# Two order changes in a fused attention and expert kernel: the sixth block product before the second, and nine memsets behind the first query halves

## The chip, the cores and the metric

The kernel runs on one core of a Trainium2 chip. The metric is the device time of one execution in microseconds (us). Engines are named as in the profile: PE is TensorE's matmul, PEld its weight load, DVE is VectorE, ACT is ScalarE, POOL is GpSimd, SP is SyncE. Each of them works its own queue of instructions in order and waits on semaphores for the others.

## What is computed

A block-sparse attention feeds a mixture of eight experts whose gate is normalised by eight Sinkhorn rounds.

```python
# attention: batch 4, heads 8, sequence 768, head size 64; block 32, window 16
k_sum = k.reshape(B, H, nb, block, D).max(axis=3)
v_sum = v.reshape(B, H, nb, block, D).mean(axis=3)
scores_l = where(|pos_q - pos_k| < window, scale * q @ k.T, -1e9)
scores_s = scale * q @ k_sum.T + log(block)
a = softmax(concat(scores_l, scores_s))
x = a @ concat(v, v_sum)                     # then laid out as 3072 x 512
# experts: 8 of them, 512 -> 1024 -> 512
P = exp(x @ w_gate - max)
for _ in range(8):
    P /= P.sum(1); P /= P.sum(0); P *= N / E
out = sum over e of P[:, e] * (relu(x @ w1[e]) @ w2[e])
```

## The kernel before

**Attention stage.** The work is cut into 16 pairs of heads, four to a batch. Pairs 0 to 3 (batch 0) are further cut into two halves of the queries. For each of these, POOL loads keys, the first half of the queries and values (`load_pair`, L256, L274, L268). PE transposes keys (`tr`, L296) and queries (`tr_qh`, L283); ACT or DVE copies the result out of PSUM (L195); DVE takes key maxima by block (`key_max`, L312); PE sums the values by block (`block_sums`, L326), and DVE copies these (`block_out`, L333); PE makes scores (`scores_h`, L318), ACT their exponentials (L442), DVE masks them (`masks_h`, L447 and L452); PE makes scores against the key maxima (`summaries`, L404), ACT their exponentials (L425). PE then multiplies with the values (`values_h`, L463), DVE takes the reciprocal of the sums (L493) and normalises (L494), PE transposes to `xT` (`to_xT`, L501) and ACT or DVE copies that (L195). Pairs 4 to 15 do the same for whole pairs, with `E_e` and `V_e` as operands for the keys near a tile's edge; SP copies the near values into `V_e` (`near_values`, L346 and L348).

The order of all this is not written out. Each step is a `Unit` with its engine, a cost in us, what it depends on and a priority, and `Plan.order` builds the program from them: it goes forward in its own time, and on each engine takes the unit that can start first, the lower priority number first where several can. The costs are constants in the source (`add("DVE", 1.6, late_constants, ...)`), and the order it makes is fixed in the program. Until expert 0's first result the plan also fills long PE waits with pairs of idle matmuls (`keep_busy`, L539).

`late_constants` (L588 to L593) is one such unit. It holds nine memsets on DVE: the two `E_e` tiles, the two `V_e` tiles with two small ones each, and `col_en`, the matrix that sums columns over partitions in the Sinkhorn rounds. It has priority 5.5, behind pairs 0 to 3's first halves (0 to 3) and ahead of the second halves (10 to 13).

Expert 0 is done without block products, as filler for PE (`expert0`: hidden products L199, projections L204), as soon as all four pairs of a batch (of batch 0: of one half) are in `xT`. Its units have the highest priority numbers. The gate (`gate`, L515 and L519) follows each batch. After the last batch come the Sinkhorn rounds (L1056 to L1077, their matmul at L1069), with the first groups of expert 1 and the last of expert 0 beside them.

**Steady period.** For experts 1 to 7 both layers are split two by two and done with seven block products in place of eight, with sums of blocks made beforehand on DVE (`x_sum`, `w1_sum`, `w2_sum`). Layer 1 works in groups (expert e, 512 of the 1536 tokens of a half, 128 of the 512 hidden columns of a half): `group` gives its steps, p1 to p7 on PE (L867, two matmuls of 512 columns each) and what is done with them. Layer 2 works in pairs (`pair`), q1 to q7 on PE (L873, four matmuls of 256 columns each), four groups behind. A step's result is accumulated in PSUM and copied to start another, so the steps wait for each other:

```python
def seed(): B["g"] = ...; nc.scalar.copy(out=B["g"][:], in_=B["a"][:])     # after p1
def c5():   B["c5"] = ...; nc.scalar.copy(out=B["c5"][:], in_=B["b"][:])   # after p5
def p6():   product1(e, i, j, B["g"], "S2", "T2", False)
def c2():   B["c2"] = ...; nc.scalar.copy(out=B["c2"][:], in_=B["g"][:])
def p2():   product1(e, i, j, B["a"], "A12", "B21", False)
def r11():  relu("ACT", h[:, A11, :], B["a"][:])
def c12():  plus(h[:, A21, :], B["b"][:], B["c2"][:])                      # after p3
def p7():   product1(e, i, j, B["g"], "S3", "T3", False)                   # after c2
```

p6 and p2 both need the seed. p7 accumulates on bank g, so it has to wait until c2 has copied it. The order of the period is written out by hand, as a list of `do(...)` calls in the main loop (n over groups, 80 periods). By engine it comes to:

- PE: q1 p1 p5 q5 p2 p6 q6 p3 p7 q2 q4 q3 p4 q7
- ACT: r21 (of the group before), c1 (L980), seed (L886), c5 (L894), r11 (L190), c2 (L901), v6 (L992); for expert 1 also two scalings (`scale0`, L965), with one operation on POOL behind them (L967)
- DVE: ya, yb of the pair before (L1010), v5 (L817, xy), s4 (L814), in some periods the sums for later groups, then c12 and c22 (L817, hf from pb and pg), r12 (L928), r22 (L931), s1 (L817), s3 and s2 (L814)

s3 needs r11's and r12's results; q6 needs v5; p3 needs c5; p4 needs c22; q3 and q7 need v6. The first four groups are in the plan of the attention stage (`bridge`) and have an order of their own.

Of the kernel before, what the change touches and what calls it, by code (L numbers as in the profile page):

```python
# [33 lines left out]
class Plan:  # L34
# [12 lines left out]
    def add(self, eng, cost, fn, deps=(), prio=0.0, opens=(), uses=(), lag=0.0):  # L47
        u = Unit(eng, cost, fn, [d for d in deps if d is not None], prio, list(opens), lag)
        for b in list(opens) + list(uses):
            b.users.append(u)  # L50
        if uses and eng != "PE":
            u.prio -= 100.0
        self.waiting.append(u)
        return u
# [62 lines left out]
def kernel(  # L117
# [21 lines left out]
    PB = H // 2  # L139
# [31 lines left out]
    def load_w1(e, i):  # L171
        t = w1s[e, i] = wpool.tile([128, KD, 2, 128], FP16, tag="w1", name="w1", bufs=5)
        for h in range(2):
            f = h * (F // 2) + 128 * i
            nc.gpsimd.dma_start(out=t[:, :, h, :],  # L175
                                in_=moe_w1[e].rearrange("(dk p) f -> p dk f", p=128)[:, :, f:f + 128])
# [7 lines left out]
    def load_w2(e):  # L184
        w2s[e] = wpool.tile([128, KF, DM], FP16, tag="w2", name="w2")
        nc.gpsimd.dma_start(out=w2s[e][:], in_=moe_w2[e].rearrange("(fk p) d -> p fk d", p=128))
# [34 lines left out]
    if True:  # L221
# [16 lines left out]
        add = plan.add  # L238
# [357 lines left out]
        U = {}  # L596
# [52 lines left out]
        def pair_half(i, h, prio):  # L649
            if h:  # L650
                query_half(i, 1, prio)
            n = PB * h + i
            hold = U["A", PB - 1, 0] if h else None
            buf = Buffer("s")
            U["S", i, h] = add("PE", 0.36, lambda: scores_h(i, h),
                               [U["kT", i, 0], U["kT", i, 1], hist("mk", n - 3), hold], prio, opens=[buf])
            U["X", i, h] = add("ACT", 1.0, lambda: score_exp_h(i, h), [U["S", i, h]], prio, uses=[buf])
            U["mk", i, h] = add("DVE", 0.78, lambda: masks_h(i, h),
                                [U["X", i, h], U["band"], hist("A", n - NEH)], prio)
            tag = "a" if h else "m"  # L660
            buf = Buffer(tag)
            U["ss", i, h] = add("PE", 0.22, lambda: summaries(i, h, tag),
                                [U["km", i], U["kT", i, 1], hist("A", n - 2), hold], prio, opens=[buf])
            U["sx", i, h] = add("ACT", 0.46, lambda: summary_exp(i, h), [U["ss", i, h]], prio, uses=[buf])
            buf = Buffer("a")
            U["A", i, h] = add("PE", 0.65, lambda: values_h(i, h),
                               [U["mk", i, h], U["sx", i, h], U["Vs", i]], prio, opens=[buf])
            U["no", i, h] = add("DVE", 0.68, lambda: normalize(i, h), [U["A", i, h], hist("xt", n - 2)],
                                prio, uses=[buf])
            buf = Buffer("a")  # L670
            U["xt", i, h] = add("PE", 0.18, lambda: to_xT(i, h), [U["no", i, h]], prio, opens=[buf])
            U["x", i, h] = add({"ACT": 0.46, "DVE": 0.5}, 0, lambda: x_out(U["x", i, h].on, i, h),
                               [U["xt", i, h]], prio, uses=[buf])
# [37 lines left out]
        def expert0(t0, xs):  # L711
            key, n = t0, len(halves)
            halves.append(key)
            pr = 1000.0 + n
            w = [U["w1", i] for i in range(2)]
            evac, old = [], [U.get(("pj", halves[n - 2], c)) for c in range(HG)] if n >= 2 else []
            for f in range(KF):
                buf = Buffer("m")

                def fn(f=f):  # L720
                    at["hp", key, f] = hidden0(key, t0, f)
                m = U["hd", key, f] = add("PE", 0.67, fn, xs + [w[f // 4]] + old, pr + f * 0.01, opens=[buf])

                def ev(f=f):
                    relu(U["rl", key, f].on, at["h", key][:, f, 0:HS], at.pop(("hp", key, f))[:, 0:HS])
                U["rl", key, f] = add({"ACT": 0.5, "DVE": 0.56}, 0, ev, [m], -1.0, uses=[buf])
                evac.append(U["rl", key, f])
                zero.extend([m, evac[-1]])
            for c in range(HG):
                buf = Buffer("m")  # L730
                p0 = add("PE", 0.88, lambda c=c: project0(key, c, 0), evac[0:4] + [U["w2"]],
                         pr + 0.1 + c * 0.02, opens=[buf])
                p1 = add("PE", 0.88, lambda c=c: project0(key, c, 1), evac[4:8] + [p0],
                         pr + 0.11 + c * 0.02, uses=[buf])
                U["pj", key, c] = p1

                def ev(c=c):
                    copy(U["yo", key, c].on, out_acc[:, t0 // 128 + c, :], at.pop(("yp", key, c))[:])
                U["yo", key, c] = add({"ACT": 0.58, "DVE": 0.68}, 0, ev, [p1], -1.0, uses=[buf])
                zero.extend([p0, p1, U["yo", key, c]])  # L740
# [23 lines left out]
        for i in range(PB):  # L764
            pair_start(i, i)
            pair_half(i, 0, i)
        add("DVE", 1.6, late_constants, [U["mk", 0, 0]], 5.5)
        expert0(0, [U["x", i, 0] for i in range(PB)])
        for i in range(PB):
            pair_half(i, 1, 10 + i)  # L770
# [28 lines left out]
    if True:  # L799
# [27 lines left out]
        def x_sum(j, n):  # L827
            m = {w: moving1(w, j) for w in "B11 B12 B21 B22 T1 T2 T3 T4".split()}
            sub(*[m[w] for w in (("T1", "B12", "B11"), ("T2", "B22", "T1"), ("T3", "B22", "B12"),
                                 ("T4", "B21", "T2"))[n]])  # L830
# [15 lines left out]
        def w1_sums(e, i):  # L846
            for n in range(4):
                w1_sum(e, i, n)
# [8 lines left out]
        def w2_sum(e, n):  # L857
            if n == 0:
                ws2[e] = extra[0].tile([128, 3, FH, DH], FP16, tag="ws2", name="ws2", bufs=2)
            m = {w: moving2(w, e) for w in "B11 B12 B21 B22 T1 T2 T3 T4".split()}  # L860
            sub(*[m[w] for w in (("T1", "B12", "B11"), ("T2", "B22", "T1"), ("T3", "B22", "B12"),
                                 ("T4", "T2", "B21"))[n]])
# [277 lines left out]
        for n in range(LAG, len(groups)):  # L1140
            g0, q0 = g, q
            g = group(*groups[n])
            q = pair(*groups[n - LAG])
            e, j, i = groups[n]
            later = e + 1 < E

            def do(*names):
                for nm in names:
                    f = g.get(nm) or q.get(nm)
                    if f is not None:  # L1150
                        f()

            def do0(*names):
                for nm in names:
                    f = g0.get(nm) or q0.get(nm)
                    if f is not None:
                        f()

            if j == 1 and i == 1 and later:
                load_w2(e + 1)  # L1160
                load_w1(e + 1, 0)
            do("q1", "p1")
            do0("r21")
            do("c1", "seed")
            do0("ya", "yb")
            do("p5", "c5")
            if n == LAG:
                w2_sum(1, 0)
                w2_sum(1, 1)
            do("q5", "v5")  # L1170
            do0("s4", "fin")
            if n == LAG:
                w2_sum(1, 2)
                w2_sum(1, 3)
            do("p2", "r11")
            if n < 2 * LAG:
                x_sum(2, n - LAG)
            if j == 2 and i > 1 and later:
                w1_sums(e + 1, i - 2)
            if e > 1 and j == 0 and i < 2:  # L1180
                w1_sums(e, i + 2)
            if j == 2 and i < 2 and later:
                w2_sum(e + 1, i)
            if e > 1 and j == 0 and i > 1:
                w2_sum(e, i)
            do("p6", "c2")
            do("q6", "v6")
            do("p3", "c12")
            do("p7", "c22", "r12")
            do("q2", "q4", "q3")  # L1190
            do("r22", "s1", "s3", "p4", "s2", "q7")
            if groups[n - LAG][0] == 1:
                do("scale0")
            if j == 2 and i < 3 and later:
                load_w1(e + 1, i + 1)
# [53 lines left out]
```

The softmax here doesn't subtract the row's maximum and nothing guards it: scores larger than these inputs give would overflow.

## Time and profile before

| what | value |
|---|---|
| median of 4 runs | 686.23 us (685.9 to 686.6) |
| profiled execution | 686.6 us, span of the core 684.9 us |
| PE | busy 671.9 us (98% of the span), 5191 matmuls |
| DVE | 590.5 us (86%) |
| ACT | 406.7 us (59%) |
| POOL | 134.5 us (20%) |
| chain that ended last | PE 85%, DVE 11%, issue 2%, DMA 1% |
| mean granted TensorE clock | 0.996 |
| first hidden product of expert 0 | 27.06 us |
| first product of the steady loop | 175.4 us |

The span is the time from the first to the last instruction of the core; the execution is 1.7 us longer. A matmul's row in a timeline shows its start and a modelled end; matmuls overlap, so distances between starts tell more than busy shares. A row of the timeline gives start, length, engine, line, operation and tiles; in square brackets stands the idle time of the engine before it, and what ended that.

### The profile page before, as it was taken

Reading aid. Unit: us, or ns where it says so; the run is one execution under the profiler, and the core shown is the slowest. Engines: PE = TensorE matmul, PEld = TensorE weight load, DVE = VectorE, ACT = ScalarE, POOL = GpSimd, SP = SyncE. Lnnn points to the kernel's source line nnn. Section 1 sums busy time; section 2 is a strip of 40 time slices with the busy share of each in tenths; the row PEclk is TensorE's granted clock in tenths of the full one; section 3 lists DMA queues with packets and bytes.
Section 4 is the critical chain, followed back from the end, with each engine's and each line's share of the span. In section 5 each row is a group of like instructions: output and inputs, shape, how many; then the busy total and the mean of one; then the engine's idle time right before and its main releaser. Section 6 shows DMA issues by size and latency. Waiting matters only on the chain.

```text
span 684.9 us, 13584 instructions
## 1 busy us (share of the span) xinstructions
PE 671.9 (98%) x5191; PEld 439.1 (64%) x5191; DVE 590.5 (86%) x1445; ACT 406.7 (59%) x784; POOL 134.5 (20%) x177
## 2 busy tenths in 40 slices
PE   7999999999999999999999999999999999999996
PEld 4666665545666666666666666666666666666665
DVE  6879988688699997999889988998899888998886
ACT  4677877555677765555555555555555555555551
POOL 8699720122203120100101010201010101100000
PEclk9999999999999999999999999999999999999999
DMA  9999990000324013220513050403131051301224
GB/s 115 190 143 142 117 124 7 1 1 0 53 26 42 7 23 56 24 24 1 78 16 32 1 78 1 48 1 57 22 31 17 7 72 16 33 1 47 78 93 154
DMA packets 113617, 33.90 MB, mean 50 GB/s; under 512 B 99984, under 2 KB 110736, under 8 KB 113552
## 3 DMA queue, kind: packets, MB, share of 16 engines
q0 software_dynamic: 104672, 26.22, 40.6%
q1 hardware_dynamic: 8352, 6.80, 3.3%
q8 instruction: 41, 0.67, 0.4%
q14 instruction: 24, 0.20, 0.1%
q10 hardware_dynamic: 528, 0.02, 0.0%
HBM read 52.45 MB, written 6.29 MB: 86 GB/s over the span
## 4 chain that ended last, share of the span: by engine, by line
PE 85%; DVE 11%; issue 2%; DMA 1%; POOL 0%; ACT 0%; DVEq 0%; ACTq 0%
PE xy L873 32%; PE pg L867 14%; PE pb L867 10%; PE pa L867 9%; PE yps L204 6%; PE hps L199 6%; DVE hf L817 3%; DVE out_acc L1010 2%; PE tkq L299 1%; PE sg L318 1%; DVE hf L928 1%; DMA vx<-in_v_dram 1%; DVE hf L814 1%; PE tx L501 1%; PE vs L326 1%
## 5 line engine op out<-in xcount | busy, mean ns | idle before, releaser
L873 PEld LDWEIGHTS <-hf 128*128 128x128 f16 x2352 | 229.7, 98 | 99.3 <-issue 5.3
L873 PE MATMUL xy<-w,hf 128*128 128x256 f16 x1312 | 183.3, 272 | 0.0
L873 PE MATMUL xy<-ws,hf 128*128 128x256 f16 x984 | 147.6, 272 | 1.5
L190 ACT ACTIVATE hf<-pg 128x512 f16<-128x512 f32 x84 | 50.2, 597 | 158.1 <-PE pg L867 158.1
L1010 DVE SCALAR_TENSOR_TENSOR out_acc<-xy,P_sb,out_acc 128x512 f32<-128x512 f32 x164 | 115.0, 743 | 1.7 <-PE xy L873 1.7
L814 DVE TENSOR_TENSOR hf<-hf 128x512 f16<-128x512 f16 x252 | 98.9, 420 | 2.9
L867 PE MATMUL pa<-xT,w 128*128 128x512 f16 x336 | 99.9, 379 | 0.0
L817 DVE TENSOR_TENSOR hf<-pb,c 128x512 f16<-128x512 f32 x84 | 57.9, 689 | 35.6 <-ACT xy L992 31.5
L867 PEld LDWEIGHTS <-w 128*128 128x128 f16 x672 | 65.6, 98 | 28.9 <-issue 0.3
L175 POOL DMA_DIRECT2D w<-in_moe_w_dram x56 | 41.9, 760 | 185.6 <-PE pg L867 157.3
L867 PEld LDWEIGHTS <-ws 128*128 128x128 f16 x504 | 49.3, 98 | 41.9
L190 ACT ACTIVATE hf<-pa 128x512 f16<-128x512 f32 x84 | 50.1, 597 | 19.2 <-PE pa L867 18.9
L817 DVE TENSOR_TENSOR hf<-pg,c 128x512 f16<-128x512 f32 x84 | 57.0, 679 | 0.1
L886 ACT COPY pg<-pa 128x512 f32<-128x512 f32 x84 | 47.9, 570 | 4.8
L867 PE MATMUL pg<-xTs,w 128*128 128x512 f16 x168 | 50.0, 379 | 0.1
L867 PE MATMUL pb<-xTs,ws 128*128 128x512 f16 x168 | 50.0, 379 | 0.0
L867 PE MATMUL pb<-xT,ws 128*128 128x512 f16 x168 | 50.0, 379 | 0.0
L867 PE MATMUL pg<-xTs,ws 128*128 128x512 f16 x168 | 50.0, 379 | 0.0
L894 ACT COPY c<-pb 128x512 f32<-128x512 f32 x84 | 49.8, 592 | 0.2 <-ACT pg L886 0.2
L867 PE MATMUL pg<-xT,w 128*128 128x512 f16 x168 | 49.8, 377 | 0.0
L199 PE MATMUL hps<-xT,w 128*128 128x384 f16 x256 | 49.4, 326 | 0.0
L901 ACT COPY c<-pg 128x512 f32<-128x512 f32 x84 | 48.7, 580 | 0.1
(136 smaller groups left out, 850.9 us busy)
## 6 DMA issues: line engine op xcount, KB each, us to landing
w<-in_moe_w_dram POOLq DMA_DIRECT2D x8, 1024.0 KB, 9.4
w<-in_moe_w_dram POOLq DMA_DIRECT2D x56, 128.0 KB, 3.6
out_dram<-out_acc SPq DMA_DIRECT2D x22, 256.0 KB, 2.0
qst<-in_q_dram POOLq DMA_DIRECT2D x32, 96.0 KB, 5.5
vx<-in_v_dram POOLq DMA_DIRECT2D x16, 192.0 KB, 6.3
kst<-in_k_dram POOLq DMA_DIRECT2D x24, 96.0 KB, 5.8
w<-in_moe_w_dram POOLq DMA_DIRECT2D x2, 512.0 KB, 8.7
kst<-in_k_dram POOLq DMA_DIRECT2D x4, 192.0 KB, 5.2
```

The lines of the kernel that those rows point to most:

```text
L175: nc.gpsimd.dma_start(out=t[:, :, h, :], in_=moe_w1[e].rearrange("(dk p) f -> p dk f", p=128)[:, :, f:f + 128])
L190: nc.scalar.activation(out=out, in_=in_, func=AF.Relu, bias=0.0, scale=1.0)
L199: nc.tensor.matmul(hp[:, 0:n], lhsT=w1s[e][:, dk, 128 * f:128 * (f + 1)], rhs=xT[:, dk, t0:t0 + n], start=(dk == 0), stop=(dk == KD - 1))
L204: nc.tensor.matmul(yp[:], lhsT=h[:, f, c * 128:(c + 1) * 128], rhs=w2s[e][:, f, :], start=(f == 0), stop=(f == KF - 1))
L814: nc.vector.tensor_tensor(out=out, in0=in0, in1=in1, op=ALU.subtract)
L817: nc.vector.tensor_tensor(out=out, in0=in0, in1=in1, op=ALU.add)
L867: nc.tensor.matmul(bank[:], lhsT=w[:, dk, :], rhs=x[:, dk, :], start=start and dk == 0, stop=dk == KH - 1, skip_group_check=True)
L873: nc.tensor.matmul(bank, lhsT=a(f)[:, 128 * c:128 * (c + 1)], rhs=w[:, f, :], start=start and f == 0, stop=f == FH - 1, skip_group_check=True)
L886: nc.scalar.copy(out=B["g"][:], in_=B["a"][:])
L894: nc.scalar.copy(out=B["c5"][:], in_=B["b"][:])
L901: nc.scalar.copy(out=B["c2"][:], in_=B["g"][:])
L1010: nc.vector.scalar_tensor_tensor(out=acc, in0=src, scalar=P_sb[:, t, e:e + 1], in1=acc, op0=ALU.mult, op1=ALU.add)
```

## The change

Two places. In the plan of the attention stage, `late_constants` depends on the masks of the last pair's first half (`PB` is 4) in place of the first pair's, and its cost in the plan is 2.4 in place of 1.6. In the steady loop, the calls for p6 and c2 and those for p2 and r11 change places; what lies between them (sums on DVE) stays where it is. The first groups of expert 1 in `bridge` are not touched.

```diff
         for i in range(PB):
             pair_start(i, i)
             pair_half(i, 0, i)
-        add("DVE", 1.6, late_constants, [U["mk", 0, 0]], 5.5)
+        add("DVE", 2.4, late_constants, [U["mk", PB - 1, 0]], 5.5)
         expert0(0, [U["x", i, 0] for i in range(PB)])
...
             if n == LAG:
                 w2_sum(1, 2)
                 w2_sum(1, 3)
-            do("p2", "r11")
+            do("p6", "c2")
             if n < 2 * LAG:
                 x_sum(2, n - LAG)
...
             if e > 1 and j == 0 and i > 1:
                 w2_sum(e, i)
-            do("p6", "c2")
+            do("p2", "r11")
             do("q6", "v6")
             do("p3", "c12")
             do("p7", "c22", "r12")
```

In the built program the steady part differs by the swap alone on PE and ACT (and in what s3 waits for). In the attention stage the planner makes another order of units on PE, DVE and ACT from about the second pair on; the same steps are in it, with two idle matmuls fewer. The queues of POOL and SP keep their order.

## The prediction

> **What bounds the kernel now.** I read the page first (PE busy in 98% of a 684.9 us span), then the table by stages, because a share over the whole span mixes stages with different limits.
>
> ```profile
> 0.00:15.00 15.00, 11.50 (x120) 5.93 (x120) 10.32 (x76) 6.42 (x9) 12.88 (x22) 0.98 1.18 108
> 15.00:30.00 15.00, 14.77 (x219) 9.31 (x216) 11.36 (x29) 9.39 (x16) 9.22 (x12) 0.91 1.45 196
> 30.00:60.00 30.00, 30.00 (x361) 18.90 (x358) 24.39 (x62) 23.07 (x37) 27.18 (x32) 1.00 2.30 146
> ...
> 202.00:255.00 53.00, 51.94 (x351) 34.01 (x349) 50.85 (x112) 39.60 (x77) 12.83 (x17) 1.00 0.18 18
> 255.00:300.00 45.00, 45.00 (x312) 30.40 (x311) 39.46 (x92) 24.08 (x50) 4.45 (x6) 1.00 0.38 46
> 300.00:400.00 100.00, 100.00 (x691) 67.30 (x689) 90.54 (x211) 56.13 (x116) 8.29 (x11) 1.00 0.19 22
> ```
>
> After the stretch, its length and then PE, PEld, DVE, ACT and POOL busy. There are three stages. Until about 27 us PE has holes and, for 3.4 us, half its clock: loads and a chain over all engines pace it. From 27 to 176 us it is filled with expert 0's products, so this stage ends when its work is done. In the steady period (176 to 664 us) PE has no hole after 255 us, but a little slack from 184 to 255 us, where DVE is busy 96%. The timeline of one late period:
>
> ```profile
> 405.27 0.57 ACT L886 COPY pg<-pa 128x512 f32<-128x512 f32 x1
> ...
> 405.94 0.59 PE L867 MATMUL pa<-xT,w 128*128 128x512 f16 x2
> ...
> 406.37 0.59 PE L867 MATMUL pg<-xTs,ws 128*128 128x512 f16 x2
> ...
> 407.06 0.58 ACT L901 COPY c<-pg 128x512 f32<-128x512 f32 x1
> ...
> 407.24 0.59 PE L867 MATMUL pb<-xT,ws 128*128 128x512 f16 x2
> 407.45 0.34 PEld L867 LDWEIGHTS <-w 128*128 128x128 f16 x2
> 407.54 0.38 ACT L992 COPY xy<-xy 128x256 f32<-128x256 f32 x1
> 407.69 0.59 PE L867 MATMUL pg<-xT,w 128*128 128x512 f16 x2
> ```
>
> The rows on PE are p2, p6, p3, p7. Ends are modelled and overlap, so starts count: p2 to p6 is 0.43, p3 to p7 is 0.45. p7 adds to the bank that c2 (ACT, L901) copies; c2 ends at 407.06 + 0.58 = 407.64, and p7 starts 0.05 later, the same 0.05 that q6 takes after v5 where it waits for DVE. At the trace's own resolution, the second matmul of p3 is followed after 241 ns and not 215: 25 ns lost. No other PE start in this period is late. The chain of waits in order of time shows the early periods:
>
> ```profile
> 196.64 0.43 DVE xy L817
> 197.12 0.60 PE xy L873 x4
> 197.72 0.45 PE pb L867 x2
> 198.21 0.04 issue
> 198.25 1.29 DVE hf L817 x2
> ```
>
> That is a loop: v5, q6, p3, c12 and c22, then DVE's r12 to yb, then v5 again: 6.36 us a period (191.90 to 198.25), against 6.10 later.
>
> **The steady swap.** It removes nothing and adds no arithmetic. p6 takes p2's place on PE, and c2 r11's on ACT.
>
> *Late periods.* p6 can start where p2 did: both wait for the seed (ends 405.84; 405.94 is when PE is free), and its operands were made periods ago. p6 then ends at 405.94 + 0.59 = 406.53, c2 runs 406.57 to 407.15, and p7, due at 407.67, finds it done with 0.5 to spare. The 25 ns go. There are 67 such periods from 255 to 664 us: 67 x 0.025 = -1.66 us. Next late would be q6 (0.11 above its minimum after v5) and p4 (0.20 after c22, against 0.05 needed), neither moved.
>
> *r11* ends about 0.5 later, at 407.65. Its cover: v6 behind it on ACT starts at 407.55 instead of 407.54, and q3 and q7, which need v6, come after 409; s3 reads r11's result at 410.12; pa's bank is next written at 410.74. Cost nothing.
>
> *A new wait.* The order of the built program shows that 80 s3 (DVE, L814), which waited for DVE alone, now wait for DVE and ACT: c12's wait for c2 used to cover r11, and no longer does. ACT is long done, but a second wait costs a step of DVE's sequencer. Four instructions of this kind are in the trace already; three hide it. The exposed one starts at 152.32 after an end at 152.22 (104 ns); with one wait the distance is 34 ns (188.25 to 188.29). So +0.07 each. Behind s3 on DVE stand s2, ya, yb, v5; q6 waits for v5. In late periods v5 stands 0.10 behind yb's end where 0.08 before it is possible, so 0.18 of cover, and q6 has 0.11 more: nothing. In the 12 periods from 184 to 255 us the loop above is back to back: 12 x 0.07 = +0.84 us. Bounds: 0 to +0.84; I take the exposed row. Otherwise the swap does nothing there: q6 waits for v5 and p7 has no lost 25 ns.
>
> **The memsets (late constants).**
>
> ```profile
> 9.83 0.79 DVE L588 MEMSET Ee<- 64x384 uint32 x2
> ...
> 12.43 0.20 DVE L493 RECIPROCAL rc<-av 128x6 f32<-128x6 f32 x1
> ...
> 13.58 0.50 PE L326 MATMUL vs<-vx,m_blk 128*64 128x128 bf16 x6 [1.41 <-DMA vx<-in_v_dram]
> ```
>
> Nine memsets (and their small waits) hold DVE from 9.83 to 12.40, 2.57 us. They issue no DMA, and POOL's and SP's orders are unchanged. Their readers are far: the first near-value DMA into Ve is at 36.35, col_en at 131. In the changed order they stand behind the masks of pair 3 and before pair 3's reciprocal.
>
> What they free: pair 1's key maxima ran at 13.13 though the keys were copied by 10.93; so its summaries came at 15.07, behind 12 transposes. Changed, the maxima run at 11.06, the summaries right behind the block sums (13.58, still set by the landing of v1 at 13.54), and an idle pair (1.0 us at half clock, 16.03) is gone. I walked the changed queues with this trace's durations and landings (v2 17.41, k3 17.83, v3 19.76): values of pair 1 start at 15.9 (now 16.84), pair 2 at 19.3 (20.41), pair 3 at 22.9 (24.10); pair 3's masks end at 22.75 (24.12).
>
> What they cost there: DVE is then held until 22.75 + 2.57 = 25.32, so pair 3's reciprocal runs at 25.35 (now 25.05) and its normalised tile is done at 26.14 (25.84). PE meanwhile has the second-half query transposes, scores and summaries, which it needs anyway. The first three of the four hidden matmuls read only pairs 0 to 2, so expert 0 starts at about 26.8 (27.06): -0.25 us. Bounds: -1.2 if pair 3's lead carries through; if nothing comes forward, 24.12 + 2.57 - 25.05 = +1.64, less the 0.38 between the copy's end (26.68) and 27.06: +1.3. I take -0.25, nearest the rows.
>
> *After 27 us* the planner's order differs, but PE does the same work, so only its stalls count. Now there are two pairs. At 70 us a transpose and the gate wait, 0.33 and 0.57 us over their usual spacing; the changed order has four products just before that transpose, and products, scores and transposes between it and the gate. At 131 and 138 us PE waits 2.0 us for the column sums; there both orders agree. I take -0.5, between -0.9 and, for a new stall elsewhere, +0.9.
>
> **A rule against the move.** PE has a granted clock of 0.50 from 14.25 to 17.67, after a 3.40 us stretch (10.8 to 14.2) with 1.99 busy and a longest hole of 1.41. [...] By the row, a window 58% busy is halved, so the stretch behind the moved memsets (24.5 to 27.9), with no idle matmuls and some 80% busy by my walk, is not safe: halved, it would cost half of 3.41 = +1.7. The window from 21.1 to 24.5, 93% busy, stays at 1.00, and 80% is nearer to that: 0. [...]
>
> **The sum.** -1.66 + 0.84 - 0.25 - 0.5 = -1.57. The profiled execution took 686.6 (span 684.9, 1.7 outside), the runs' median is 686.23; from that 684.66, say 684.7.
>
> **Rivals and chances.** 0.2% is 1.37 us, about what a measurement can tell; so faster means below 684.86, slower above 687.60.
>
> 1. As summed, 684.7, chance 0.52, its own spread about 0.9 (of which 0.34 below 684.86).
> 2. The lead of pair 3 carries through and the 70 us stalls go: -1.66 + 0.84 - 0.9 - 0.9 = -2.6, 683.6, chance 0.20. For it: DVE's queue is what held pair 1. Against: memsets ahead of the last pair's reciprocal.
> 3. The memsets only move the hold from pair 1 to pair 3, because loads pace the pairs: -0.82 + 1.3 - 0.3 = +0.2, 686.4, chance 0.19. For it: the 1.41 wait for v1. Against: v2 and v3 landed before PE used them.
> 4. p7's 25 ns are not c2's (the change does not do what it says): +0.84 - 0.75, 686.3, chance 0.03. Against: the 0.05 after c2's end, every period.
> 5. Slower: rival 3's gap at 24.5 to 27.9 us also halves the clock: +0.2 + 1.7 = +1.9, 688.1, chance 0.06. It decides from a window as empty as the 58% one.
>
> Faster 0.54, same 0.40, slower 0.06. The range, 683.4 to 686.5, reaches from rival 2 to rival 3.
>
> **What would show it.** Late periods of 6.075 instead of 6.10 us, with p3 to p7 at 0.43 (else the first step is wrong); early ones of 6.43 instead of 6.36 (6.36: the second wait is hidden); values of pair 3 near 22.9, its reciprocal near 25.35, the first hidden matmul near 26.8; no PE wait at 70 us; one halved clock window. Wrong altogether if q6 waits in late periods, or PE gains new holes between 27 and 125 us.

## The result and the profile after

The changed kernel takes 684.69 us (median of 33 runs, 683.89 to 688.22), the kernel before 685.86 in the 53 runs beside it (684.79 to 689.15): a ratio of 0.9983, 95% interval 0.9976 to 0.9990, or 1.2 us of gain. (The ratios here and below are those of the record, and are not quite the quotients of the medians.) Between 683.4 and 686.5 with 684.7 as the likeliest, the forecast holds; but its terms do not all. The profiled execution took 685.08 us with a span of 682.4, against 684.9 before. That difference of 2.5 us is larger than the medians', for two reasons: the execution shown before had 3.41 us of halved clock near its start, and the one after has none; and the time outside the span is not fixed (1.7 us in the one, 2.7 in the other). So below, stretches are also compared with `e0_before`, the kernel before once more, whose profiled execution has none either (span 683.4).

The table by stages, after the change (stretch, length, then PE, PEld, DVE, ACT, POOL busy, granted clock, DMA share, GB/s):

```profile
0.00:15.00 15.00, 12.24 (x139) 6.37 (x140) 9.46 (x70) 6.78 (x10) 13.01 (x22) 1.00 1.19 107
15.00:30.00 15.00, 13.41 (x223) 8.93 (x224) 13.49 (x39) 10.90 (x19) 9.10 (x12) 1.00 1.43 196
...
202.00:255.00 53.00, 51.66 (x350) 34.07 (x349) 49.55 (x111) 37.91 (x73) 12.94 (x17) 1.00 0.22 24
...
300.00:400.00 100.00, 99.92 (x690) 67.22 (x688) 89.70 (x210) 56.60 (x117) 9.24 (x12) 1.00 0.20 24
```

The clock reads 1.00 in both first rows (0.98 and 0.91 before). From 202 to 255 us PE is idle 1.34 us, where it was 1.06. And from 300 to 400 us it is no longer quite full: 0.08 us are missing, which the prediction had not foreseen.

A late period, from the timeline after:

```profile
403.19 0.57 ACT L886 COPY pg<-pa 128x512 f32<-128x512 f32 x1
...
403.85 0.59 PE L867 MATMUL pg<-xTs,ws 128*128 128x512 f16 x2
...
404.29 0.59 PE L867 MATMUL pa<-xT,w 128*128 128x512 f16 x2
...
404.54 0.59 ACT L901 COPY c<-pg 128x512 f32<-128x512 f32 x1 [0.28 <-PE pg L867]
...
405.02 0.60 ACT L190 ACTIVATE hf<-pa 128x512 f16<-128x512 f32 x1
...
405.15 0.59 PE L867 MATMUL pb<-xT,ws 128*128 128x512 f16 x2
...
405.59 0.59 PE L867 MATMUL pg<-xT,w 128*128 128x512 f16 x2
```

p6 now starts ahead of p2; c2 ends at 404.54 + 0.59 = 405.13 and p7 starts at 405.59, 0.46 later. p7 is no longer held by c2, and the period is 6.078 us (p7 to p7) where it was 6.100.

An early period in the chain of waits, after:

```profile
194.25 0.43 DVE xy L817
...
194.72 0.60 PE xy L873 x4
195.32 0.45 PE pb L867 x2
...
195.86 1.29 DVE hf L817 x2
...
200.67 0.43 DVE xy L817
```

It is the loop that was there before, v5, q6, p3, c12 and c22, and back to v5, but now 200.67 - 194.25 = 6.42 us long.

The first pairs, from the timeline after:

```profile
12.90 0.50 PE L326 MATMUL vs<-vx,m_blk 128*64 128x128 bf16 x6 [0.90 <-DMA vx<-in_v_dram]
...
21.60 0.79 DVE L588 MEMSET Ee<- 64x384 uint32 x2
...
24.19 0.20 DVE L493 RECIPROCAL rc<-av 128x6 f32<-128x6 f32 x1
...
25.07 0.33 PE L501 MATMUL tx<-ident,xs 128*128 128x128 f16 x3 [0.58 <-ACT es L425]
25.66 1.47 PE L199 MATMUL hps<-xT,w 128*128 128x384 f16 x8
```

The memsets stand at 21.60 and hold pair 3's reciprocal until 24.19, as walked in the prediction but 1.2 us earlier: in this execution the clock was whole, and the values of pair 1 came 0.7 us sooner. PE then waits 0.58 us for pair 3's transposes; the releaser named is an exponential, but what these transposes read is the normalised tile, which DVE makes only after the reciprocal.

At 70 us, first the kernel before, then the changed one:

```profile
70.28 0.51 PE L501 MATMUL tx<-ident,xs 128*128 128x128 f16 x6 [0.17 <-DVE xs L494]
...
71.67 0.74 PE L515 MATMUL lp<-wg_bf,xT 128*128 128x8 f16 x24 [0.24 <-ACT xT L195]
```

```profile
69.62 0.82 PE L199 MATMUL hps<-xT,w 128*128 128x384 f16 x4
70.53 0.38 PE L318 MATMUL sg<-qT,kT 64*128 64x160 bf16 x6
...
71.53 0.74 PE L515 MATMUL lp<-wg_bf,xT 128*128 128x8 f16 x24
```

The two waits in brackets are gone from the changed kernel; other work stands there, with one smaller hole in it: four hidden products take 0.65 us where they follow each other (0.16 each), and the scores start 0.91 after the first of them.

Where the time went, by PE's starts in the profiled executions (us; the loop begins with the first product of layer 2 in it, at 175.20 in the kernel before and not at 175.4):

| stretch | before | e0_before | after | after - e0_before | predicted |
|---|---|---|---|---|---|
| to the first hidden product | 27.06 | 25.49 | 25.66 | +0.17 | -0.25 |
| from there to the loop | 148.14 | 148.14 | 146.98 | -1.16 | -0.5 |
| early periods, 12 | 76.49 | 76.51 | 77.27 | +0.76 | +0.84 |
| late periods, 67 | 408.70 | 408.70 | 407.97 | -0.73 | -1.66 |
| span | 684.9 | 683.4 | 682.4 | -1.0 | -1.57 |

The two rows that the swap changes cancel, +0.76 and -0.73: in this kernel the whole gain is that of the order after 27 us.

### The profile page after: what moved, and what is told of

Its sections match the earlier page's. It is cut to its first block, busy times and chain, and to the rows that moved or that the text cites. A ratio compares the mean times of both kernels' runs of the same rounds, so it can differ in the third digit from the quotient of the medians.

```text
span 682.4 us, 13662 instructions
## 1 busy us (share of the span) xinstructions
PE 668.2 (98%) x5189; PEld 438.9 (64%) x5189; DVE 589.5 (86%) x1444; ACT 407.1 (60%) x785; POOL 134.7 (20%) x177
## 4 chain that ended last, share of the span: by engine, by line
PE 83%; DVE 12%; issue 2%; DMA 1%; POOL 1%; ACT 1%; DVEq 0%; ACTq 0%
PE xy L873 32%; PE pg L867 14%; PE pb L867 10%; PE pa L867 9%; PE yps L204 6%; PE hps L199 6%; DVE hf L817 3%; DVE out_acc L1010 2%; PE tkq L299 1%; PE sg L318 1%; DVE hf L814 1%; DVE hf L928 1%; DVE xy L817 1%; DMA vx<-in_v_dram 1%; PE vs L326 1%
```

## The experiments

The theory after the result: three terms are real and separate, p7's relief, s3's second wait, and a better order of PE's work after 27 us, with nothing gained ahead of it; the halved clock comes and goes by itself. The rivals: the gain is the prologue's and the clock's; the better order comes from one half of the memset line alone; s3 is not what lengthens the early periods. Two findings of the first runs added questions of their own: three periods with a new wait, and what starts the halved clock. A time is the median of a kernel's runs; the kernel before ran beside each.

### e0_before: the kernel before, again

No edit.

> The kernel before, unchanged, to see how its executions spread in clock and span. If the half-clock stretch of its profile (14.3 to 17.7 us) belongs to its order, every execution has a mean clock near 0.996 and a span near 684.9, and the profile shows 0.50 there again. [...]

Measured: 685.79 us (14 runs), ratio 1.0002 (0.9992 to 1.0012). Its timeline:

```profile
12.03 0.50 PE L326 MATMUL vs<-vx,m_blk 128*64 128x128 bf16 x6 [0.28 <-DMA vx<-in_v_dram]
...
12.70 0.94 DVE L312 TENSOR_REDUCE ksT<-kT 128x24 bf16<-128x768 bf16 x1
...
23.48 0.20 DVE L493 RECIPROCAL rc<-av 128x6 f32<-128x6 f32 x1 [0.94 <-PE av L463]
...
25.49 1.48 PE L199 MATMUL hps<-xT,w 128*128 128x384 f16 x8
```

The same kernel's values of pair 1 landed 1.55 us earlier (11.99 for 13.54), the wait for them was 0.28 instead of 1.41, no stretch ran at half clock, and expert 0 began at 25.49 instead of 27.06. So 1.57 us of the difference between the first two profiles belongs to the execution and not to the change. Pair 3's reciprocal runs at 23.48 here, ahead of the changed kernel's 24.19.

### e1_swap: the steady swap alone

```diff
-            do("p2", "r11")
+            do("p6", "c2")
...
-            do("p6", "c2")
+            do("p2", "r11")
```

> The swap alone; the memsets stay where they were. By the sum of the two traces (12 early periods +0.07 us each = +0.8; 67 late ones -0.022 each = -1.45; new q6 stalls of 0.24, three of them, +0.7 if they come with the swap) the swap is worth -0.6 to 0.0 us, a ratio of 0.999 to 1.000. Rival, that the swap is what made the kernel faster: -1.2 us, ratio 0.998.

Measured: 685.5 us (684.52 to 687.09, 14 runs), ratio 0.9991 (0.9981 to 1.0001). Early periods 6.428, the 12 of them 77.33; late periods 6.078, the 67 of them 407.46; up to the loop it is e0_before to 0.01 us. In periods, the swap is worth 407.46 - 408.70 = -1.24 late and 77.33 - 76.51 = +0.82 early. (One late period, at 364 us, is 0.21 longer than the others.) That leaves -0.4, less than the interval of the ratio tells from nothing.

### e2_memsets: the memset line alone

```diff
-        add("DVE", 1.6, late_constants, [U["mk", 0, 0]], 5.5)
+        add("DVE", 2.4, late_constants, [U["mk", PB - 1, 0]], 5.5)
```

> The memsets' move alone, the steady loop as before. If the gain is the attention stage's: the loop starts 1 to 2.6 us earlier (first p7 of the loop at 176 to 177.5 instead of 178.7), late periods stay at 6.100, early ones at 6.356; ratio 0.997 to 0.9985. If the swap made the gain: ratio 1.000.

Measured: 685.02 us (684.16 to 688.39, 14 runs), ratio 0.9997 (0.9984 to 1.0011). First hidden product at 25.38, from there to the loop 146.99: the better order is the memset line's, and it comes with the steady loop as it was. But the 67 late periods take 409.40 where the same loop took 408.70, which eats most of it. Three single periods are longer, by 0.22, 0.28 and 0.20, at 385, 515 and 595 us, though the change lies ahead of 30 us. e7_one_more looks for the cause.

### e3_late_swap: the memsets, and the swap where it helps

```diff
+            swap = groups[n - LAG][0] > 1
-            do("p2", "r11")
+            do(*(("p6", "c2") if swap else ("p2", "r11")))
...
-            do("p6", "c2")
+            do(*(("p2", "r11") if swap else ("p6", "c2")))
```

> The memsets moved, and p6 ahead of p2 only in the 68 periods whose second layer belongs to expert 2 or later; the 12 periods of expert 1 keep p2 first. If the second wait of s3 is what lengthens the early periods, these are 6.356 again and late ones 6.078: 0.8 us less than the changed kernel, ratio to before about 0.997. If the early periods are longer for another reason of the move (the planner's other order before them), they stay at 6.425 and the time equals the changed kernel's, 0.9983.

Measured: 683.59 us (682.75 to 684.59, 6 runs), ratio 0.9966 (0.9952 to 0.9979). Early periods back at 6.359, the 12 of them 76.41; late ones 6.078 and all 67 of them: 407.25, which is 67 x 6.078. It is faster than the kernel before, and by the medians 1.1 us faster than the changed one. Its profiled execution had a stretch of half clock (16.77 to 20.18), with the same memset line that shows none in the changed kernel's: the same order of work has it in one execution and not in another.

### e4_cost_only and e5_dep_only: the two halves of the memset line

In both the steady loop is that of before. e4 has the new cost with the old dependency, e5 the old cost with the new dependency:

```diff
+        add("DVE", 2.4, late_constants, [U["mk", 0, 0]], 5.5)        (e4)
+        add("DVE", 1.6, late_constants, [U["mk", PB - 1, 0]], 5.5)   (e5)
```

> Steady loop as before; the memsets stay behind pair 0's masks, only their cost in the plan is 2.4 in place of 1.6. In the built order the place that waits at 70 us has the same work in front of it as before. Theory A (the moved dependency is what makes the planner's better order after 27 us): from the first hidden product to the loop 148.1 us as in the kernel before, with the two waits at 70 us, total 685.5 to 685.9. Theory B (the truer cost makes it): 147.0, without these waits, total about 684.9. Periods 6.356 and 6.100 in both.

> Steady loop as before; the memsets stand behind pair 3's masks, their cost in the plan stays 1.6. Theory A (the moved dependency makes the better order): 147.0 us from the first hidden product to the loop, no wait at 70 us, total 684.7 to 685.0. Theory B (the truer cost does): 148.1, total 685.5 to 685.9. Periods 6.356 and 6.100 in both; the first hidden product at 25.4 to 25.7 if no half-clock stretch falls into the execution, 1.7 later if one does.

Measured: e4 687.85 us (20 runs), ratio 1.0026 (1.0018 to 1.0034); e5 687.33 us (12 runs), ratio 1.0012 (1.0 to 1.0024). Both medians lie above the kernel before, e5's at the edge of its interval, and neither theory had that. A part of it is common to both: their late stretch takes 409.40, with three longer periods, as e2_memsets' does (+0.70). The rest differs. e4 keeps the two waits at 70 us (0.17 and 0.24, as in the kernel before), begins expert 0 at 26.69, and has a new wait ahead of the loop:

```profile
175.79 0.60 PE L873 MATMUL xy<-w,hf 128*128 128x256 f16 x4 [0.67 <-ACT out_acc L195]
```

From the first hidden product to the loop it takes 149.1 us. So the truer cost alone makes a worse order: PE's order in the plan shifts, and the place at 70 us is not mended. Why expert 0 begins later was not followed. e5 loses its time elsewhere. Two of its rows by stretches of 3.41 us, and one row of its timeline:

```profile
23.25:26.66 3.41, 1.92 (x38) 1.23 (x31) 2.31 (x11) 2.22 (x4) 2.95 (x4) 1.00 1.24 207
26.67:30.07 3.40, 3.40 (x28) 1.72 (x27) 2.26 (x5) 0.87 (x2) 0.43 (x1) 0.50 1.50 193
```

```profile
26.26 0.34 PE L501 MATMUL tx<-ident,xs 128*128 128x128 f16 x3 [1.09 <-DVE xs L494]
```

Here the memsets stand at 22.82 to 25.4. The plan counts them as 1.6 us where they take 2.6, and puts pair 3's transposes where their operand is not yet made: PE waits 1.09 us. The stretch from 23.25 is 56% busy and the next one has half the clock. That is the prediction's fifth case to the letter (the hold moves to pair 3, and the gap halves the clock), on a kernel with half of the memset line. From the first hidden product to the loop e5 takes 148.56; its part at half clock, 27.65 to 30.08, costs about 1.2 of these (an estimate, half of its 2.43 us), so the order itself stands near 147.3. It has no waits at 70 us, but it is not the changed kernel's order either: there is a new wait of 0.50 us at 73 us, and of the two waits for the column sums (0.78 and 0.93 us in e0_before) one is left, of 0.61. So the dependency takes the waits at 70 us away and the cost does not; how much of the changed kernel's order each half brings is not separated. What the cost does for the memsets can be read: behind them PE waits 1.09 us in e5 and 0.58 in the changed kernel, whose attention stages differ by it alone. The clock makes most of e5's loss: its three runs with a mean clock of 0.999 take 685.72 to 685.88 us, as the kernel before does (685.89), and the nine others, at 0.997 or less, 686.86 to 688.86.

### e7_one_more: a memset more, for the count

The changed kernel has three late periods of 6.319 us in place of 6.078. One of them in its timeline, with the group's row on its page:

```profile
324.16 0.60 PE L873 MATMUL xy<-ws,hf 128*128 128x256 f16 x4
...
325.22 0.43 DVE L817 TENSOR_TENSOR xy<-xy,c 128x256 f32<-128x256 f32 x1 [0.36 <-PE pg L867]
...
325.70 0.60 PE L873 MATMUL xy<-ws,hf 128*128 128x256 f16 x4
```

```profile
L873 PE MATMUL xy<-ws,hf 128*128 128x256 f16 x984 | 147.6, 272 | 2.3 <-DVE xy L817 1.8
```

One period earlier v5 starts 0.71 us after q5; here it is 1.06, with DVE free, and q6 waits for it. (The group's idle time was 1.5 before and is 2.3 now.) The distance between these three periods is 146.1 us, 24 periods, and in the trace v5 is record 831, 1215 and 1599 of DVE: always 63 above a multiple of 128. DVE's waits that stand alone are records of their own (record 830 is the wait of v5 at 831), and s3's second wait is one such; with it the period has 16 records on average instead of 15, and 24 periods have 384, three times 128. The test shifts all records by a step:

```diff
             nc.vector.memset(warm, 0.0)
+            nc.vector.memset(warm, 0.0)
```

> The changed kernel with one more tiny memset on DVE at the start, so that every later DVE record has another number. Theory A (DVE's issue pauses of 0.4 us belong to every 128th record, and cost time only where that record follows a wait): the three q6 waits of 0.24 at 325, 471 and 617 us go, or move to other records; the 67 late periods take 407.3 to 407.5 in place of 408.0, the total 0.5 to 0.7 less than the changed kernel's. Theory B (they belong to v5 in those periods, whatever its number): still three waits of 0.24, total as the changed kernel's, 684.7.

Measured: 683.68 us (683.14 to 687.24, 11 runs), ratio 0.9970 (0.9955 to 0.9986). Late periods 407.25, none longer; early ones 77.34 as in the changed kernel. The same period in its timeline:

```profile
324.49 0.60 PE L874 MATMUL xy<-ws,hf 128*128 128x256 f16 x4
325.19 0.43 DVE L818 TENSOR_TENSOR xy<-xy,c 128x256 f32<-128x256 f32 x1
...
325.79 0.60 PE L874 MATMUL xy<-ws,hf 128*128 128x256 f16 x4
```

One tiny memset more, and 0.72 us in the late stretch less. The waits belong to the number of the record.

The same count explains every long late period of the other kernels. Over all of them there are 20 that are 0.20 to 0.28 us longer: 15 with a DVE record of that number behind a stand-alone wait, and 5 with an ACT record of that number, in e2_memsets this one (record 831 of ACT, c2), which holds p7:

```profile
514.44 0.58 ACT L901 COPY c<-pg 128x512 f32<-128x512 f32 x1 [0.17 <-ACT hf L190]
515.07 0.59 PE L867 MATMUL pg<-xT,w 128*128 128x512 f16 x2
```

### e8_filled: idle matmuls where PE waits for values

e3_late_swap, with four matmuls of zeros ahead of pair 1's block sums, in the bank that these overwrite:

```diff
-            vs = at["vs", i] = bank("a", "vs")[0:64, 0:2 * D]
+            full = bank("a", "vs")
+            for _ in range(4 if i == 1 else 0):
+                nc.tensor.matmul(full[:], lhsT=zeros[:], rhs=zeros[...], start=True, stop=True)
+            vs = at["vs", i] = full[0:64, 0:2 * D]
```

> The memsets moved and the swap in experts 2 to 7 only, and four idle matmuls of 512 columns on PE ahead of pair 1's block sums, where PE waits for the values to land. Theory A (a hole of over 1.3 us in that wait lets the clock be halved in some executions): the longest hole before the first hidden product is under 1.0 us, no half-clock stretch, total 682.8 to 683.6. Theory B (the halved clock has another cause): half-clock executions as often as without the idle matmuls, total about 683.6, or later where the idle work delays the block sums.

Measured: 683.14 us (682.54 to 683.47, 6 runs), ratio 0.9948 (0.9933 to 0.9964), the lowest median of this study (the intervals of e8_filled and e3_late_swap overlap). The two stretches that were the emptiest elsewhere:

```profile
9.95:13.36 3.41, 3.41 (x52) 1.95 (x51) 2.73 (x6) 1.99 (x3) 3.41 (x5) 1.00 1.55 145
13.37:16.78 3.41, 3.33 (x63) 2.41 (x62) 2.68 (x7) 1.97 (x4) 3.03 (x5) 1.00 1.88 166
```

None of its 6 runs and none of e10's 21 has a mean granted clock of 0.997 or less; 7 of the changed kernel's 35 recorded ones, 9 of e5's 12 and 29 of the 141 runs of the kernel before that were timed beside the experiments have. The idle matmuls cost little that the profile shows (first hidden product at 26.16, against 25.38 to 26.15 in the kernels of the same order at full clock).

### e9_act_old and e11_act_new: what lengthens the early periods

Both separate PE's order from ACT's in expert 1's periods. e9 is the changed kernel with ACT's old order in them; e11 is e3_late_swap with ACT's new order in them:

```diff
+            old = groups[n - LAG][0] == 1                                   (e9)
+            do(*(("p6",) if old else ("p6", "c2")))
...
+            do(*(("p2", "r11", "c2") if old else ("p2", "r11")))
```

```diff
+            do(*(("p6", "c2") if swap else ("p2",)))                        (e11)
...
+            do(*(("p2", "r11") if swap else ("p6", "c2", "r11")))
```

> The changed kernel, but in expert 1's periods ACT does r11 ahead of c2 again, while PE keeps p6 ahead of p2. By the built order s3 then waits for DVE alone in these periods, as before the change. Theory A (s3's second wait, on ACT, is the price of the early periods): 6.356 to 6.36 us in place of 6.425, the 12 periods 76.4 to 76.5 in place of 77.3, total 0.8 less than the changed kernel's. Theory B (p6 ahead of p2 on PE, or c2's place, is the price): 6.42 to 6.43. Late periods 6.078 in both; the three q6 waits stay, since DVE has as many instructions as in the changed kernel.

> The memsets moved and the swap in experts 2 to 7, as in e3_late_swap; in expert 1's periods PE keeps p2 ahead of p6, but ACT does c2 ahead of r11. By the built order s3 then waits for DVE and ACT in these periods, and c2 comes no later than before. Theory A (the second wait is the price of the early periods): 6.42 to 6.43 us, the 12 periods 77.2 to 77.4, with 0.10 from s1's end to s3's start; total 0.8 over e3_late_swap. Theory B (p6 ahead of p2 on PE is the price): 6.356 to 6.36, the 12 periods 76.4 to 76.5, 0.03 from s1 to s3 or the 0.10 hidden.

e9 measured: 684.98 us (22 runs), ratio 0.9989 (0.9979 to 0.9999). Its early periods are 6.532 us, above what either theory said. The timeline names the reason:

```profile
228.20 0.60 ACT L190 ACTIVATE hf<-pa 128x512 f16<-128x512 f32 x1 [0.66 <-PE pa L867]
228.70 0.58 ACT L901 COPY c<-pg 128x512 f32<-128x512 f32 x1
...
229.31 0.69 DVE L817 TENSOR_TENSOR hf<-pb,c 128x512 f16<-128x512 f32 x1 [0.21 <-ACT c L901]
```

p2 ends later than p6 now, so r11 starts later, c2 queues behind it, and c12 waits for c2. As a test of the second wait by the total, e9 says nothing; its rows of s1 and s3 speak for it, since with one wait the distance is 0.03 us:

```profile
224.55 0.83 DVE L817 TENSOR_TENSOR hf<-hf 128x512 f16<-128x512 f16 x1
225.41 0.76 DVE L814 TENSOR_TENSOR hf<-hf 128x512 f16<-128x512 f16 x2
```

e9 missed on the late stretch too: 407.25, with no longer period, because DVE has 12 records fewer by then.

e11 measured: 684.67 us (683.62 to 688.48, 20 runs), ratio 0.9978 (0.9965 to 0.9991). The 12 early periods take 77.31. s1 and s3 in its timeline, then in that of e0_before:

```profile
227.06 0.42 DVE L817 TENSOR_TENSOR hf<-hf 128x512 f16<-128x512 f16 x1
227.59 1.10 DVE L814 TENSOR_TENSOR hf<-hf 128x512 f16<-128x512 f16 x2
```

```profile
224.41 0.43 DVE L817 TENSOR_TENSOR hf<-hf 128x512 f16<-128x512 f16 x1
224.87 0.76 DVE L814 TENSOR_TENSOR hf<-hf 128x512 f16<-128x512 f16 x2
```

From s1's end to s3's start it is 0.11 us with two waits, 0.03 with one. (That s3 and s2 take 1.10 here and 0.76 there is no part of it: r12 takes 0.28 here and 0.85 there. In the kernel before, r12 takes its 0.85 from 224.89, while POOL's operation on the result for expert 1 runs from 224.86 to 225.58.) At the trace's own resolution the distance is 34 ns in the early periods of before, e0, e3 and e9, and 104 or 105 ns in those of after, e1, e7 and e11; in e1_swap all other steps of the loop on DVE are as long as in e0_before. PE's order was the old one in e11, so the price of the early periods is s3's second wait. The late stretch takes 407.97 us with longer periods at the same three places as the changed kernel: DVE has the same number of records again. Two builds with the same count, one outcome; three with other counts (e3, e7, e9), the other.

e11's profiled execution also had the longest stretch at half clock, 14.63 to 24.87 us, after the emptiest stretch of all:

```profile
11.22:14.63 3.41, 1.81 (x25) 1.01 (x21) 1.75 (x6) 1.35 (x2) 3.40 (x6) 1.00 1.64 152
```

### e10_filled_old: e8_filled with the memsets where they were

```diff
-        add("DVE", 2.4, late_constants, [U["mk", PB - 1, 0]], 5.5)
+        add("DVE", 1.6, late_constants, [U["mk", 0, 0]], 5.5)
```

> The memsets back where they were, the swap in experts 2 to 7 only, and four idle matmuls on PE ahead of pair 1's block sums; beside e8_filled this differs by the memsets alone. Theory A (the moved memsets are worth the better order after 27 us, and nothing ahead of it): first hidden product within 0.3 of 25.5 to 26.2, from there to the loop 148.1 against 147.0, total 1.1 us over e8_filled, 684.2 to 684.4. Theory B (they are worth more, since DVE holds pair 1's summaries): the first hidden product later than e8_filled's 26.16 by over 0.5, total 684.8 or more. Half-clock stretches as rare as in e8_filled if the filled hole is what allows them.

Measured: 685.02 us (684.28 to 686.1, 21 runs), ratio 0.9982 (0.9974 to 0.9989), 1.9 over e8_filled. First hidden product at 25.39, 0.77 earlier than e8_filled's: the moved memsets gain nothing there. From it to the loop 148.14, that is +1.15 as expected. The early periods take 76.51 against 76.41. The rest is the late stretch: 408.14 against 407.25, in three places like this one, and in a fourth at 363 us, behind c2 (record 575 of ACT):

```profile
284.56 0.69 DVE L821 TENSOR_TENSOR hf<-pb,c 128x512 f16<-128x512 f32 x1 [0.73 <-PE pg L871]
```

The three are records 703, 1087 and 1471 of DVE, again 63 above a multiple of 128, now at c12. So a part of e10's loss is the count of its records, and not the memsets' place; the first theory's 684.2 to 684.4 missed by that. These terms make 1.4 us, the difference of the two profiled spans (682.7 and 681.3); the other 0.5 of the medians is not explained.

## Why the prediction was right, step by step

**The late periods, -1.66 expected, -1.45 for the step itself.** p7 was held by c2, and is not any more: from p3's second matmul to p7 it is 240 to 243 ns in every late period before, and 215 or 216 in every one after. The 25 ns were read from one gap in one period (67 x 0.025 is 1.68 and not 1.66); 3 of them come back elsewhere, since the periods differ by 6.100 - 6.078 = 22 ns, and e3_late_swap, with no long period, has 407.25 - 408.70 = -1.45. The mechanism was right. What the sum lacked stands beside it: three periods in the changed kernel are 0.24 longer, +0.72, so -0.73 was left. The prediction had named "q6 waits in late periods" as the sign of being wrong, and q6 does wait in three of them; but for another reason than any it gave. It came from s3's new wait, as a record in DVE's queue and not by its 70 ns. The sum had put that at nothing.

**s3's second wait, +0.84 expected, +0.76 measured.** The exposed row, 104 ns against 34, was the right one to choose. e11_act_new shows the same 0.11 with PE's old order. In the late periods it is hidden, as the 0.18 of cover said: they are as long in e3_late_swap and e7_one_more, both with the second wait, as the relief of p7 makes them. The periods grew by 6.425 - 6.356 = 0.069.

**The prologue, -0.25 expected, no gain measured.** Against e0_before it is +0.17. At full clock all the way, the first hidden product starts at 25.38 to 26.16 in the five kernels with this memset line (e2, after, e7, e9, e8; mean 25.85) and at 25.39 to 25.49 in the three with the old one (e0, e1, e10; mean 25.46): no gain, and perhaps a loss of 0.4, one profile each. The walk was right in its order (pair 3's values forward, its reciprocal behind the memsets), but it was made with the landings and the halved clock of one execution, and called the result the change's. What pair 3 gained, its reciprocal's wait behind the memsets took back: it runs at 24.19, against 23.48 in e0_before, and PE waits 0.58 at 25.07.

**After 27 us, -0.5 expected, -1.16 measured.** The waits at 70 us are gone, as forecast, but they were smaller than the 0.33 and 0.57 of the prediction: in e0_before the last product of a pair's summaries is followed after 0.27 us at other places of this stretch too, so only 0.30 of the gate's 0.57 is wait. With two delays of 0.14 beside them and the new hole of 0.25 at 70.5 this place gives -0.66. The other -0.5 was not foreseen: PE has the same 1424 matmuls in this stretch, and the saving is spread over many small distances between their starts; what makes it was not separated. (The two idle matmuls fewer have no part in it, since all of them stand ahead of the first hidden product.) e4 and e5 show how thin this ice is: with either half of the same line alone the median is 1.4 to 2 us above the kernel before, 0.7 of it by the count of records, and in e5 most of the rest by the clock.

**The clock, 0 expected for the new gap, and "one halved clock window" expected.** No halved stretch follows the moved memsets: the stretch before 24.8 us was 79% busy, close to the 80% of the walk. But the one window that was forecast to stay is absent in the profile after. It comes in some executions of a kernel and not in others, and in some kernels oftener (a mean granted clock of 0.997 or less in 9 of e5's 12 runs, in 7 of the changed kernel's 35). In 13 profiles of this study, cut into the 3.41 us in which the clock's records change, the share in which PE was busy by the profile tells them apart: the stretches at 0.59 (before), 0.61 (e3), 0.64 and 0.56 (e5) and 0.53 (e11) were each followed by half the clock, and of the other stretches at full clock between 7 and 670 us, at 0.65 (e9), 0.66 (e0) and up, none was. The longest single hole in any of those up to 28 us is 1.60 us. The share does not tell them apart everywhere: where the kernel ends, from 675 us, stretches at 0.43 (e9) and 0.44 (e0) were not followed by half the clock, while 0.36 (e1) and 0.40 (e3) were. In two of the five a single wait for values was all that PE was idle in the stretch: 1.41 us of 3.41 in the kernel before, 1.60 in e11. The phase of these windows differs from execution to execution (one begins at 10.84 before and at 10.73 in e0, at 11.15 after and at 13.35 in e3), and so do the landings, so the same kernel falls on either side, as before and e0 do. The filled kernels, 27 runs without a low clock, are the test by hand: with the wait filled, it stayed away.

**The sum.** -1.57 from four terms; they measured +0.17, -1.16, +0.76, -0.73, -1.0 in span and -1.17 in the medians. The forecast was met by a gain after 27 us twice as large as put down, and a late stretch that kept half of its gain. The steady swap, put down as -0.82, came to nothing. That the likeliest time, 684.7, is the measured one is luck: it was counted from 686.23, the median of 4 runs, where 53 runs give 685.86. So the prediction was right in its two mechanisms of the steady loop and in the place at 70 us, and in its total by the balance of misjudged sizes.

## What to carry to other kernels

Where a hand-written order is swapped, look at what each instruction waited for and what covered it: the gain was 22 ns in 67 periods, and all of it went back through one new wait on another engine, half in the 12 periods where that engine is the bound and half as one record more in its queue. So use the swap only where the engine it relieves is the bound (e3_late_swap, 1.1 us under the changed kernel by the medians), and give a planner the true cost of a step along with its place, since neither alone gained here. Before reading a prologue's gain from two profiles, profile the same kernel twice; and if PE's share of a window of 3.41 us falls as low there as it did here ahead of each halved clock up to 28 us (0.53 to 0.64, where none followed 0.65 and more), try to fill the hole with idle matmuls.

## What was not expected of the hardware

**DVE and ACT paused at some of every 128th record.** In these profiles an instruction whose number among its engine's records in the trace is 63 above a multiple of 128, and which directly follows a stand-alone wait, mostly starts late. In the late stretches of the 13 profiles DVE has 19 such records: 15 start 0.416 to 0.435 us after the wait's start where 0.066 is usual, and the other four, in sums of weights, show no delay. ACT has 14: c2 starts after 0.336 us where 0.057 is usual (five times), c5 after 0.75 where 0.48 is usual (four times), and v6 and r11 show no delay (five times). Where the record before it is an operation instead, nothing is to be seen (record 703 of DVE after the change, s1, starts 0.319 us after the one before it, as s1 does in the other periods). In the late loop the pause was worth 0.2 to 0.3 us a time and up to 0.9 in all, as much as the changes that this study was about; an edit anywhere ahead of it, of one instruction (e7_one_more's memset) or of one wait (s3's), turned it on or off.

The trace has something beside these records. The page of the changed kernel lists two DMA queues of the kind "instruction" (packets, MB, share):

```profile
q8 instruction: 40, 0.66, 0.4%
q14 instruction: 26, 0.21, 0.1%
```

The packets of the second are 8 KB each. From 258 to 660 us it moves 15 of them in each of the 13 profiles, one in 27 us; DVE, ACT and POOL have 14 records of that number there, and every one of these has a packet within 4.6 us, ahead of it or behind it. So records and packets lie near each other in time; whether the packets have to do with the pause, and why it shows only behind a wait, the runs do not show.

**A halved clock for three windows.** After e11's emptiest stretch the clock stayed at 0.50 for 10.24 us, although PE was busy in all of it; after the other four it came back after 3.41. It is one case, so whether the depth of the fall decides this is open.
